# Fused pooled attention and branch mixture: other queues and order for the first keys and queries, and tile 1 done like tile 0

## The chip, the cores and the metric

The kernel runs on one NeuronCore of a Trainium2 chip. The metric is the device time of one execution in microseconds (us), lower is better. The profile gives a span, from the first to the last instruction of the core; the time of an execution is some 2 us longer.

## The reference

```python
# attention: q, k, v of shape (8, 8, 576, 64); keys and values are averaged over 8 neighbours
k_p = k.reshape(B, H, 72, 8, D).mean(axis=3)
v_p = v.reshape(B, H, 72, 8, D).mean(axis=3)
scores = (1 / sqrt(D)) * q @ k_p.transpose(0, 1, 3, 2)
attn = exp(scores - max(scores));  attn = attn / (sum(attn) + 1e-9)
x = (attn @ v_p)                       # -> (4608, 512): tokens by heads * head_dim
# mixture: 4 experts, w1 (4, 512, 1024), w2 (4, 1024, 512), p of shape (4608, 4)
p = domain_probs / (domain_probs.sum(-1) + 1e-9)
out = sum over e of p[:, e] * (relu(x @ w1[e]) @ w2[e])
```

## The kernel before

The 4,608 tokens are cut into 36 tiles of 128, four tiles to a group of 512. For each group and expert there is a step: `up` multiplies the group's turned tokens `xT` with one expert's `w1` (eight blocks of 128 columns, ReLU on ScalarE), and `down` multiplies the result, tile by tile, with `w2`; `collect` scales it on VectorE and adds it up. The main loop over 36 steps puts `up` of the next step between the `down` of this one, in an order written out by hand (`SLOTS`, `plan`), with the attention of later groups placed in its slots. Each engine runs its instructions in the order of the program.

Ahead of that loop stands a head, also in an order written out by hand, which makes the attention of group 0 (tiles 0 to 3) and the first expert's products for it. Its parts:

- `qg` (L129): the queries of all four tiles, 1 MB in F32, loaded by SP. `split_q(c)` (L565) casts one tile to BF16 on ScalarE, `turn_q` (L301) transposes it on TensorE and ScalarE copies it to `qT`. Tile `c` of group 0 holds every fourth token.
- `load_rows` (L77) loads the first keys into `kraw[0]` on GpSimd's queue, which casts to BF16, in three parts; `fold_keys0` (L581) adds eight neighbours on VectorE in three steps, `turn_keys0` transposes on TensorE, `take_keys0` (L601) copies into `kT[0]`. `load_v(0)` and then the weights follow on the same queue.
- `scores` (L316), `less_max` (L343: maxima and difference on VectorE), `expo` (L349, ScalarE).
- Tile 0 goes "in rows": `expo` writes `attn` unnormalised, `attn_T` (L387) transposes it and a copy makes `attnT`; `sums0` (L631) forms the sums over each head by products with the constant `own`; `context_rows` (L404) makes the context with tokens in partitions, and its division by the sums writes `x_sb`; `turn_x0` (L645) transposes it, and ScalarE copies it to `xT`.
- Tiles 1 to 3: `normalise` (L377) sums and divides on VectorE ahead of `attn_T`, and `context` (L424) gives `xT` turned.
- `up_tile(s, i)` (L460) is the up-projection for one tile alone, in two halves of 16 products.
- `idle_products(n)` (L569) runs `n` products on a tile of zeros whose result is not used.
- `own` and `ident` are made on GpSimd; `mask_v` (L184) is spread from `own` on VectorE.

PSUM pools hold two buffers each (`ps_h`, `ps_o`, `ps_t`) or one (`ps_s`, the scores), so a writer waits until the reader of an older tile is done.

The order of the head after the keys is:

```python
    take_keys0()
    make_mask_v()
    scores(0)
    split_q(2)
    turn_q(2)
    less_max(0)
    split_q(3)
    expo(0)
```

Of the kernel before, what the change touches and what calls it, by code (L numbers as in the profile page):

```python
# [10 lines left out]
ALU = mybir.AluOpType  # L11
AX = mybir.AxisListType
BF16 = mybir.dt.bfloat16
# [4 lines left out]
def kernel(  # L18
# [58 lines left out]
    def load_rows(dst, src, parts=((0, NB - 1),)):  # L77
        rows = src.rearrange("h (j r) d -> (h j) (r d)", r=POOL)
        for i0, i1 in parts:
            nc.gpsimd.dma_start(  # L80
                out=dst[:, i0:i1, :],
                in_=rows[i0 * P:i1 * P].rearrange("(i p) x -> p i x", p=P),
            )
        nc.gpsimd.dma_start(out=dst[0:TAIL, NB - 1, :], in_=rows[(NB - 1) * P:ROWS])
# [4 lines left out]
    def load_v(b):  # L89
        load_rows(vraw[b % 2], v[b])  # L90
# [22 lines left out]
    def load_w1(e):  # L113
        for half in range(2):
            cols = slice(half * (F // 2), (half + 1) * (F // 2))
            nc.gpsimd.dma_start(
                out=w1_sb[e][:, :, cols],
                in_=moe_w1[e].rearrange("(kc p) f -> p kc f", p=P)[:, :, cols],
            )

    def load_w2(e):
# [4 lines left out]

    qg = raw.tile([P, H, TPG, D], F32, name="qg")  # L129
    nc.sync.dma_start(  # L130
        out=qg[:], in_=q[0][:, 0:G, :].rearrange("h (p c) d -> p h c d", c=TPG)
    )
    dp0 = const.tile([P, TPG, E], F32, name="dp0")
    nc.sync.dma_start(
        out=dp0[:], in_=moe_domain_probs[0:G].rearrange("(p c) e -> p c e", c=TPG)
# [6 lines left out]

    still = const.tile([P, G], BF16, name="still")
    nc.vector.memset(still[:], 0.0)  # L144
    load_rows(kraw[0], k[0], ((0, 2), (2, 4)))
    load_v(0)
    ident = const.tile([P, P], BF16, name="ident")
    make_identity(nc, ident[:])

# [2 lines left out]
    for sign, base in ((1, 0), (-1, SP - 1)):  # L152
        nc.gpsimd.affine_select(
            out=own[:], in_=own[:], compare_op=ALU.is_ge, fill=0.0,
            base=base, channel_multiplier=sign,
            pattern=[[sign * (P - PW), NPAIR], [sign * P, 2], [-sign * SP, 2]],
        )
    load_w1(0)
    load_w2(0)
    load_w1(1)  # L160
# [133 lines left out]
    def by_dma(t):  # L294
        return t >= 2 * TPG


    def in_rows(t):
        return t == 0 or by_dma(t)

    def turn_q(t):  # L301
        qT[t] = qtp.tile([P, NPAIR, P], BF16, name="qT")
# [98 lines left out]

    def context_rows(t):  # L404
        ps = ps_t.tile([P, DM], F32, tag="t", name="x_ps")
        for b, _, n, at in segments(t * P, P):
            flat = vbd[b][:].rearrange("p a z y d -> p (a z y d)")
            for i in range(NB):
                c0, c1, h0 = chunk(i)
                nc.tensor.matmul(  # L410
                    ps[at:at + n, h0 * D:(h0 + c1 - c0) * D],
                    lhsT=attnT[t][:, i, at:at + n], rhs=flat[:, c0 * D:c1 * D],
                    start=(i == 0), stop=(i == NB - 1), skip_group_check=True,
                )
        x_sb = soft.tile([P, DM], BF16, name="x_sb")
        nc.vector.scalar_tensor_tensor(  # L416
            out=x_sb[:].rearrange("p (h d) -> p h d", d=D),
            in0=ps[:].rearrange("p (h d) -> p h d", d=D), scalar=V_MEAN,
            in1=rss[t][:].unsqueeze(2).to_broadcast([P, H, D]),
            op0=ALU.mult, op1=ALU.mult,  # L420
        )
        return x_sb

    def context(t):  # L424
        g, col = t // TPG, (t % TPG) * P
        if t % TPG == 0:
            xT[g] = grp.tile([P, KC, G], BF16, name="xT")
        if by_dma(t):
            x_sb = x_sbs[t] = context_rows(t)
            nc.sync.dma_start_transpose(out=xT[g][:, :, col:col + P], in_=x_sb[:])  # L430
            return
        ps = ps_t.tile([P, KC, P], F32, tag="t", name="x_ps")
        for pair in range(NPAIR):
            for b, _, n, at in segments(t * P, P):
                for z in range(2):
                    nc.tensor.matmul(  # L436
                        ps[:, pair, at:at + n],
                        lhsT=vbd[b][:, pair, z].rearrange("p y d -> p (y d)"),
                        rhs=attnT[t][:, pair + z, at:at + n],
                        start=(z == 0), stop=(z == 1),  # L440
                    )
        nc.scalar.copy(out=xT[g][:, :, col:col + P], in_=ps[:])  # L442
# [14 lines left out]
        nc.scalar.activation(out=hs[s][:, fb, :], in_=ps[:], func=ACT.Relu)  # L457


    def up_tile(s, i):  # L460
        g, e = divmod(s, E)
        if i == 0:
            hs[s] = hpool.tile([P, FB, G], BF16, name="h_sb")
        cols = slice(i * P, (i + 1) * P)
        for f0 in range(0, FB, TPG):
            ps = ps_h.tile([P, TPG, P], F32, tag="h", name="h_ps")
            for f in range(TPG):
                for kc in range(KC):
                    nc.tensor.matmul(  # L469
                        ps[:, f], lhsT=w1_sb[e][:, kc, (f0 + f) * P:(f0 + f + 1) * P],  # L470
                        rhs=xT[g][:, kc, cols], start=(kc == 0), stop=(kc == KC - 1),
                    )
            nc.scalar.activation(
                out=hs[s][:, f0:f0 + TPG, cols], in_=ps[:], func=ACT.Relu
            )
# [87 lines left out]


    def split_q(c):  # L565
        nc.scalar.copy(out=qrow[c][:], in_=qg[:, :, c, :])


    def idle_products(n):  # L569
        ps = ps_o.tile([P, DM], F32, name="o_ps")  # L570
        for _ in range(n):
            nc.tensor.matmul(ps[:], lhsT=still[:, 0:P], rhs=still[:], start=True, stop=True)  # L572
# [7 lines left out]

    def fold_keys0(p1, i0, i1):  # L581
        rows = kraw[0][0:p1, i0:i1]
        for n in (4, 2):
            w = n * D
            nc.vector.tensor_add(
                out=rows[:, :, 0:w], in0=rows[:, :, 0:w], in1=rows[:, :, w:2 * w]
            )
        twice = [p1, i1 - i0, 2, D]
        nc.vector.tensor_tensor(
            out=kpad0[0:p1, i0:i1], in0=rows[:, :, 0:D].unsqueeze(2).to_broadcast(twice),  # L590
            in1=rows[:, :, D:2 * D].unsqueeze(2).to_broadcast(twice), op=ALU.add,
        )
# [35 lines left out]
            )  # L628


    def sums0():  # L631
        ps = ps_o.tile([P, H], F32, tag="o_ps", name="es_ps")
        flat = own[:].rearrange("p a z y -> p (a z y)")
        for i in range(NB):
            c0, c1, h0 = chunk(i)
            nc.tensor.matmul(
                ps[:, h0:h0 + c1 - c0], lhsT=attnT[0][:, i], rhs=flat[:, c0:c1],
                start=(i == 0), stop=(i == NB - 1), skip_group_check=True,
            )
        es = soft.tile([P, H], F32, name="es")  # L640
        nc.vector.tensor_scalar_add(out=es[:], in0=ps[:], scalar1=1e-9)
        rss[0] = soft.tile([P, H], F32, name="rs")
        nc.vector.reciprocal(out=rss[0][:], in_=es[:])

    def turn_x0(x_sb):  # L645
        ps = ps_t.tile([P, KC, P], BF16, tag="t", name="xT_ps")
        for kc in range(KC):
            nc.tensor.transpose(ps[:, kc], x_sb[:, kc * P:(kc + 1) * P], ident[:])
        nc.scalar.copy(out=xT[0][:, :, 0:P], in_=ps[:])

    idle_products(14)
    split_q(0)
    split_q(1)
    turn_q(0)
    turn_q(1)
    for part in ((P, 0, 2), (P, 2, 4), (TAIL, 4, 5)):
        fold_keys0(*part)
        turn_keys0(*part)
        idle_products(2)
    take_keys0()  # L660
    make_mask_v()
    scores(0)
    split_q(2)
    turn_q(2)
    less_max(0)
    split_q(3)
    expo(0)
    idle_products(2)
    spread_values0(sum_values0())
    attn_T(0)  # L670
    scores(1)
    maxima(1)
    idle_products(2)
    sums0()
    turn_q(3)
    idle_products(1)
    xT[0] = grp.tile([P, KC, G], BF16, name="xT")
    x0 = context_rows(0)
    idle_products(4)
    turn_x0(x0)  # L680
    less(1)
    expo(1)
    idle_products(2)
    up_tile(0, 0)
    scores(2)
    normalise(1)
    idle_products(4)
    less_max(2)
    domain_probs0()
    for t in range(1, TPG):  # L690
        attn_T(t)
        if t + 1 < TPG:
            expo(t + 1)
        if t == 1:
            idle_products(3)
        else:
            down(0, t - 1, 0, FB // 2)
        context(t)
        if t == 1:
            scores(3)  # L700
            up_tile(0, t)
            down(0, t - 1)
        else:
            down(0, t - 1, FB // 2, FB)
            up_tile(0, t)
        if t + 1 < TPG:
            normalise(t + 1)
        if t == 1:
            less_max(3)
        if t == TPG - 1:  # L710
            make_mask_k()
        collect(0, t - 1)
    load_q(2 * TPG)
# [48 lines left out]
```

## Time and profile before

| what | value |
|---|---|
| median of 3 runs | 552.44 us (552.02 to 552.67) |
| profiled execution, its own time | 551.91 us |
| its span | 549.9 us |
| TensorE busy | 537.4 us, 98% |
| tile 0's `attnT` copy starts | 15.38 us |
| up-projection of tile 0, of tile 1, main loop's first product | 19.05, 24.45, 36.87 us |

All times are counted from the span's start. In the profile PE is TensorE's products, PEld its weight loads, DVE VectorE, ACT ScalarE, POOL GpSimd, SP the SyncE queue that starts transfers. Numbers such as L453 are lines of the kernel; those in the prediction are lines of the kernel before. A row of the timeline reads: start, duration, engine, line, operation, output and input, count.

### The profile page before, as it was taken

To read this page: it belongs to the slowest core of one execution; us is meant where nothing else is said; L and a number is where in the kernel's file an instruction comes from. 1 tells how busy PE (TensorE), PEld (TensorE's weight loads), DVE (VectorE), ACT (ScalarE), POOL (GpSimd) and SP (SyncE) were. 2 spreads that over 40 slices of the span, in tenths; PEclk is the share of its full clock that TensorE was granted. 3 is DMA by queue.
4 is the path that set the end of the run, shared out by engine and by line. 5 is a ranking of instruction groups with operands and counts; after the bars stand their busy time and mean duration, and the time that the engine had idled before them with its cause. 6 is when DMAs were issued, how large, how long until landed. Compare 5 with 4: busy or idle time off the path is not lost.

```text
span 549.9 us, 7267 instructions
## 1 busy us (share of the span) xinstructions
PE 537.4 (98%) x2873; PEld 260.8 (47%) x2929; DVE 264.7 (48%) x456; ACT 213.5 (39%) x355; POOL 70.7 (13%) x120
## 2 busy tenths in 40 slices
PE   7899999999999999999999999999999999999997
PEld 2664554444444444444444444444444444444443
DVE  4874847444744446544554444744473444422223
ACT  3554653333333333333333333333333333333330
POOL 7234001121111100012011100101010000000000
PEclk9999999999999999999999999999999999999999
DMA  9999926556645563367435543335333521111002
GB/s 196 206 202 198 201 19 130 83 67 88 119 72 76 79 121 73 52 83 91 110 54 76 83 108 39 52 42 114 45 54 41 92 57 32 21 39 38 1 1 76
DMA packets 110689, 45.84 MB, mean 83 GB/s; under 512 B 87584, under 2 KB 106016, under 8 KB 110656
## 3 DMA queue, kind: packets, MB, share of 16 engines
q0 software_dynamic: 51472, 22.03, 32.6%
q1 hardware_dynamic: 59184, 23.35, 17.9%
q8 instruction: 23, 0.38, 0.3%
q14 instruction: 10, 0.08, 0.0%
HBM read 45.16 MB, written 9.44 MB: 99 GB/s over the span
## 4 chain that ended last, share of the span: by engine, by line
PE 96%; DMA 1%; DVE 1%; issue 1%; ACT 1%; POOL 0%; POOLq 0%
PE o_ps L486 45%; PE h_ps L453 44%; PE x_ps L410 2%; PE sc L320 2%; PE h_ps L469 1%; DMA kraw<-in_k_dram 1%; PE x_ps L436 1%; PE o_ps L572 0%; PE at_ps L394 0%; ACT attnT L395 0%; PE qT_ps L310 0%; POOL kraw L80 0%; DVE mx L334 0%; DVE d_sb L338 0%; DVE acc L501 0%
## 5 line engine op out<-in xcount | busy, mean ns | idle before, releaser
L457 ACT ACTIVATE h_sb<-h_ps 128x512 bf16<-128x512 f32 x280 | 167.1, 597 | 296.5 <-PE h_ps L453 292.3
L453 PE MATMUL h_ps<-xT,w 128*128 128x512 bf16 x1088 | 271.8, 379 | 1.5
L486 PE MATMUL o_ps<-w,h_sb 128*128 128x512 bf16 x1130 | 270.0, 379 | 1.3
L486 PEld LDWEIGHTS <-h_sb 128*128 128x128 bf16 x1152 | 112.4, 98 | 133.8
L501 DVE SCALAR_TENSOR_TENSOR acc<-o_ps,p_sb,acc 128x512 f32<-128x512 f32 x108 | 81.0, 750 | 180.4 <-PE o_ps L486 177.7
L453 PEld LDWEIGHTS <-w 128*128 128x128 bf16 x1120 | 105.9, 98 | 116.9
L497 DVE TENSOR_SCALAR acc<-o_ps,p_sb 128x512 f32<-128x512 f32 x36 | 27.0, 750 | 60.8 <-PE o_ps L486 60.8
L525 POOL COPY gated<-x_sb 1x1 bf16<-1x1 bf16 x28 | 7.8, 278 | 367.7 <-DVE x_sb L416 367.7
L108 POOL DMA_DIRECT2D qrow<-in_q_dram x36 | 30.5, 850 | 26.3 <-DMA w<-in_moe_w_dram 14.8
L334 DVE TENSOR_REDUCE mx<-sc 128x8 f32<-128x576 f32 x36 | 27.2, 756 | 10.8 <-PE sc L320 10.6
L338 DVE TENSOR_TENSOR d_sb<-sc,mx 128x576 f32<-128x576 f32 x36 | 27.3, 757 | 1.2
L416 DVE SCALAR_TENSOR_TENSOR x_sb<-x_ps,rs 128x512 bf16<-128x512 f32 x29 | 20.1, 692 | 12.5 <-PE x_ps L410 12.1
L351 ACT ACTIVATE attn<-d_sb 128x576 bf16<-128x576 f32 x29 | 19.8, 682 | 3.7 <-DVE d_sb L338 0.5
L372 DVE TENSOR_REDUCE es<-attn 128x8 f32<-128x576 bf16 x28 | 20.8, 744 | 0.0
L410 PEld LDWEIGHTS <-attnT 128*128 128x128 bf16 (+1 forms) x160 | 12.2, 100 | 7.3 <-issue 1.3
L320 PE MATMUL sc<-kT,qT 128*128 128x144 bf16 (+1 forms) x160 | 15.0, 227 | 0.2 <-DVE kT L609 0.2
L320 PEld LDWEIGHTS <-qT 128*128 128x128 bf16 (+1 forms) x160 | 11.1, 100 | 8.4 <-issue 2.2
L410 PE MATMUL x_ps<-vbd,attnT 128*128 128x192 bf16 (+5 forms) x160 | 14.7, 231 | 0.0
L572 PE MATMUL o_ps<-still 128*128 128x512 bf16 x36 | 11.4, 435 | 1.4 <-DVE still L144 1.3
L235 DVE TENSOR_TENSOR vraw<-vraw 128x1280 bf16<-128x1280 bf16 (+1 forms) x14 | 9.2, 654 | 0.2
L235 DVE TENSOR_TENSOR kraw<-kraw 128x1280 bf16<-128x1280 bf16 (+1 forms) x14 | 9.0, 640 | 0.2
L469 PE MATMUL h_ps<-xT,w 128*128 128x128 bf16 x128 | 7.8, 219 | 0.7 <-ACT xT L442 0.4
(76 smaller groups left out, 148.8 us busy)
## 6 DMA issues: line engine op xcount, KB each, us to landing
out_dram<-acc SPq DMA_DIRECT2D x36, 256.0 KB, 2.2
vraw<-in_v_dram POOLq DMA_DIRECT2D x8, 512.0 KB, 6.7
w<-in_moe_w_dram POOLq DMA_DIRECT2D x8, 512.0 KB, 16.1
w<-in_moe_w_dram POOLq DMA_DIRECT2D x4, 1024.0 KB, 16.2
kraw<-in_k_dram POOLq DMA_DIRECT2D x7, 512.0 KB, 6.2
qrow<-in_q_dram POOLq DMA_DIRECT2D x28, 128.0 KB, 4.0
qg<-in_q_dram SPq DMA_DIRECT2D x1, 1024.0 KB, 5.8
kraw<-in_k_dram POOLq DMA_DIRECT2D x2, 256.0 KB, 6.7
```

What stands on the lines that cost most here:

```text
L108: nc.gpsimd.dma_start(out=qrow[t][at:at + n], in_=q[b][:, tok:tok + n, :].rearrange("h p d -> p h d"),)
L320: nc.tensor.matmul(sc[at:at + n, pair // 2, (pair % 2) * PW:(pair % 2 + 1) * PW], lhsT=qT[t][:, pair, at:at + n], rhs=kT[b][:].rearrange(" ...
L334: nc.vector.reduce_max(out=mxs[t][:], in_=by_head(t), axis=AX.X)
L338: nc.vector.tensor_tensor(out=st[t][:], in0=by_head(t), in1=mxs[t][:].unsqueeze(3).to_broadcast([P, 2, 4, SP]), op=ALU.subtract,)
L372: nc.vector.reduce_sum(out=es[:], in_=e, axis=AX.X)
L410: nc.tensor.matmul(ps[at:at + n, h0 * D:(h0 + c1 - c0) * D], lhsT=attnT[t][:, i, at:at + n], rhs=flat[:, c0 * D:c1 * D], start=(i == 0), s ...
L416: nc.vector.scalar_tensor_tensor(out=x_sb[:].rearrange("p (h d) -> p h d", d=D), in0=ps[:].rearrange("p (h d) -> p h d", d=D), scalar=V_ME ...
L453: nc.tensor.matmul(ps[:], lhsT=w1_sb[e][:, kc, fb * P:(fb + 1) * P], rhs=xT[g][:, kc, :], start=(kc == 0), stop=(kc == KC - 1),)
L457: nc.scalar.activation(out=hs[s][:, fb, :], in_=ps[:], func=ACT.Relu)
L486: nc.tensor.matmul(ps[:], lhsT=hs[s][:, fb, i * P:(i + 1) * P], rhs=w2_sb[e][:, fb, :], start=(fb == 0), stop=(fb == FB - 1),)
L497: nc.vector.tensor_scalar_mul(out=accs[t][:], in0=ps[:], scalar1=p_sb[:, e, t:t + 1])
L501: nc.vector.scalar_tensor_tensor(out=accs[t][:], in0=ps[:], scalar=p_sb[:, e, t:t + 1], in1=accs[t][:], op0=ALU.mult, op1=ALU.add,)
```

## The change

The first keys no longer go through GpSimd's queue: SP loads them in F32 into a new tile `kf`, the short last part first, and then the queries of tile 0 alone (`qf`). The queries of tiles 1 to 3 (`qg`) are loaded by GpSimd's queue in BF16, behind the values and ahead of the weights; the constants `ident` and `own` are made ahead of these loads. The first step of the fold reads `kf` and writes `kraw[0]`. `mask_v` is made first.

Tile 1 is done in rows too: `sums0` becomes `sums_by_products(t)`, `context_rows` can write x in two halves (two divisions on VectorE), and `turn_x0` becomes `turn_x(t, halves)`, with two transposes and a copy for each half, in two PSUM pools. `up_tile` can run one of its halves; the turn of tile 1's exponents, copied on VectorE, stands between the halves for tile 0. `scores(3)` comes after `up_tile(0, 1)`. There are 30 idle products instead of 38.

```diff
-    qg = raw.tile([P, H, TPG, D], F32, name="qg")
-    nc.sync.dma_start(
-        out=qg[:], in_=q[0][:, 0:G, :].rearrange("h (p c) d -> p h c d", c=TPG)
-    )
+    kf = raw.tile([P, NB, POOL * D], F32, name="kf")
+    rows0 = k[0].rearrange("h (j r) d -> (h j) (r d)", r=POOL)
+    nc.sync.dma_start(out=kf[0:TAIL, NB - 1, :], in_=rows0[(NB - 1) * P:ROWS])
+    for i in (0, 2):
+        nc.sync.dma_start(
+            out=kf[:, i:i + 2, :],
+            in_=rows0[i * P:(i + 2) * P].rearrange("(i p) x -> p i x", p=P),
+        )
+    q0 = q[0][:, 0:G, :].rearrange("h (p c) d -> p h c d", c=TPG)
+    qf = raw.tile([P, H, D], F32, name="qf")
+    nc.sync.dma_start(out=qf[:], in_=q0[:, :, 0, :])
...
-    load_rows(kraw[0], k[0], ((0, 2), (2, 4)))
-    load_v(0)
     ident = const.tile([P, P], BF16, name="ident")
     make_identity(nc, ident[:])
...
+    load_v(0)
+    qg = raw.tile([P, H, TPG - 1, D], BF16, name="qg")
+    nc.gpsimd.dma_start(out=qg[:], in_=q0[:, :, 1:TPG, :])
     load_w1(0)
...
     def in_rows(t):
-        return t == 0 or by_dma(t)
+        return t < 2 or by_dma(t)
...
+        x = [soft.tile([P, n * D], BF16, name=f"x_sb{i}of{parts}") for i in range(parts)]
+        for i in range(parts):
+            heads = slice(i * n, (i + 1) * n)
+            nc.vector.scalar_tensor_tensor(
...
     def split_q(c):
-        nc.scalar.copy(out=qrow[c][:], in_=qg[:, :, c, :])
+        nc.scalar.copy(out=qrow[c][:], in_=qg[:, :, c - 1, :] if c else qf[:])
...
+    def turn_x(t, halves):
+        n = KC // 2
+        for i, pool, tag in ((0, ps_t, "t"), (1, ps_h, "h")):
+            ps = pool.tile([P, n, P], BF16, tag=tag, name="xT_ps")
+            for kc in range(n):
+                nc.tensor.transpose(
+                    ps[:, kc], halves[i][:, kc * P:(kc + 1) * P], ident[:]
+                )
+            nc.scalar.copy(
+                out=xT[0][:, i * n:(i + 1) * n, t * P:(t + 1) * P], in_=ps[:]
+            )
+        idle_products(1)
```

The head's order, after the change:

```python
    idle_products(14)
    make_mask_v()
    split_q(0)
    for part in ((TAIL, 4, 5), (P, 0, 2)):
        fold_keys0(*part)
        turn_keys0(*part)
    idle_products(3)
    turn_q(0)
    fold_keys0(P, 2, 4)
    turn_keys0(P, 2, 4)
    take_keys0()
    idle_products(3)
    scores(0)
    less_max(0)
    split_q(1)
    expo(0)
    idle_products(2)
    v_ps = sum_values0()
    idle_products(1)
    turn_q(1)
    spread_values0(v_ps)
    attn_T(0)
    scores(1)
    split_q(2)
    maxima(1)
    idle_products(2)
    xT[0] = grp.tile([P, KC, G], BF16, name="xT")
    sums_by_products(0)
    x_sb = context_rows(0, 2)
    turn_q(2)
    split_q(3)
    idle_products(1)
    turn_x(0, x_sb)
    less(1)
    expo(1)
    up_tile(0, 0, (0,))
    attn_T(1, copy=nc.vector.tensor_copy)
    up_tile(0, 0, (TPG,))
    sums_by_products(1)
    x_sb = context_rows(1, 2)
    scores(2)
    turn_q(3)
    idle_products(2)
    turn_x(1, x_sb)
    less_max(2)
    expo(2)
    domain_probs0()
    up_tile(0, 1)
    scores(3)
    down(0, 0)
    normalise(2)
    less_max(3)
    collect(0, 0)
    for t in range(2, TPG):     # as before
```

More of the change, by code (lines that the diff above doesn't have):

```diff
@@ L398, in chunk, with context_rows @@
         return max(0, 4 * i - 1), min(4 * NPAIR, 4 * i + 2), max(0, 2 * i - 1)
-    def context_rows(t):
+    def context_rows(t, parts=1):
         ps = ps_t.tile([P, DM], F32, tag="t", name="x_ps")
@@ L414, in context_rows @@
                 )
[L415 to L422, printed above, removed]
+        n = H // parts
+        x = [soft.tile([P, n * D], BF16, name=f"x_sb{i}of{parts}") for i in range(parts)]
+        for i in range(parts):
+            heads = slice(i * n, (i + 1) * n)
+            nc.vector.scalar_tensor_tensor(
+                out=x[i][:].rearrange("p (h d) -> p h d", d=D),
+                in0=ps[:].rearrange("p (h d) -> p h d", d=D)[:, heads], scalar=V_MEAN,
+                in1=rss[t][:, heads].unsqueeze(2).to_broadcast([P, n, D]),
+                op0=ALU.mult, op1=ALU.mult,
+            )
+        return x
     def context(t):
@@ L428, in context @@
         if by_dma(t):
-            x_sb = x_sbs[t] = context_rows(t)
+            (x_sb,) = context_rows(t)
+            x_sbs[t] = x_sb
             nc.sync.dma_start_transpose(out=xT[g][:, :, col:col + P], in_=x_sb[:])
@@ L457, in up, with up_tile @@
         nc.scalar.activation(out=hs[s][:, fb, :], in_=ps[:], func=ACT.Relu)
-    def up_tile(s, i):
+    def up_tile(s, i, starts=tuple(range(0, FB, TPG))):
         g, e = divmod(s, E)
-        if i == 0:
+        if s not in hs:
             hs[s] = hpool.tile([P, FB, G], BF16, name="h_sb")
         cols = slice(i * P, (i + 1) * P)
-        for f0 in range(0, FB, TPG):
+        for f0 in starts:
             ps = ps_h.tile([P, TPG, P], F32, tag="h", name="h_ps")
@@ L582, in fold_keys0 @@
         rows = kraw[0][0:p1, i0:i1]
+        src = kf[0:p1, i0:i1]
         for n in (4, 2):
@@ L585, in fold_keys0 @@
             nc.vector.tensor_add(
-                out=rows[:, :, 0:w], in0=rows[:, :, 0:w], in1=rows[:, :, w:2 * w]
+                out=rows[:, :, 0:w], in0=src[:, :, 0:w], in1=src[:, :, w:2 * w]
             )
+            src = rows
         twice = [p1, i1 - i0, 2, D]
@@ L628, in spread_values0, with sums_by_products @@
             )
-    def sums0():
+    def sums_by_products(t):
         ps = ps_o.tile([P, H], F32, tag="o_ps", name="es_ps")
@@ L636, in sums0 @@
             nc.tensor.matmul(
-                ps[:, h0:h0 + c1 - c0], lhsT=attnT[0][:, i], rhs=flat[:, c0:c1],
+                ps[:, h0:h0 + c1 - c0], lhsT=attnT[t][:, i], rhs=flat[:, c0:c1],
                 start=(i == 0), stop=(i == NB - 1), skip_group_check=True,
@@ L641, in sums0 @@
         nc.vector.tensor_scalar_add(out=es[:], in0=ps[:], scalar1=1e-9)
[L642 to L649, printed above, removed]
+        rss[t] = soft.tile([P, H], F32, name="rs")
+        nc.vector.reciprocal(out=rss[t][:], in_=es[:])
@@ L651 @@
+    def turn_x(t, halves):
[8 more added lines that the diff above has]
+                out=xT[0][:, i * n:(i + 1) * n, t * P:(t + 1) * P], in_=ps[:]
+            )
+        idle_products(1)
     idle_products(14)
+    make_mask_v()
@@ L652 @@
     split_q(0)
[L653 to L656, printed above, removed]
+    for part in ((TAIL, 4, 5), (P, 0, 2)):
         fold_keys0(*part)
         turn_keys0(*part)
-        idle_products(2)
+    idle_products(3)
+    turn_q(0)
+    fold_keys0(P, 2, 4)
+    turn_keys0(P, 2, 4)
     take_keys0()
-    make_mask_v()
+    idle_products(3)
     scores(0)
-    split_q(2)
-    turn_q(2)
     less_max(0)
-    split_q(3)
+    split_q(1)
     expo(0)
     idle_products(2)
-    spread_values0(sum_values0())
+    v_ps = sum_values0()
@@ L670 @@
+    idle_products(1)
+    turn_q(1)
+    spread_values0(v_ps)
     attn_T(0)
     scores(1)
+    split_q(2)
     maxima(1)
     idle_products(2)
-    sums0()
-    turn_q(3)
+    xT[0] = grp.tile([P, KC, G], BF16, name="xT")
+    sums_by_products(0)
+    x_sb = context_rows(0, 2)
+    turn_q(2)
+    split_q(3)
     idle_products(1)
[L677 to L680, printed above, removed]
+    turn_x(0, x_sb)
     less(1)
     expo(1)
+    up_tile(0, 0, (0,))
@@ L683 @@
+    attn_T(1, copy=nc.vector.tensor_copy)
+    up_tile(0, 0, (TPG,))
+    sums_by_products(1)
+    x_sb = context_rows(1, 2)
+    scores(2)
+    turn_q(3)
     idle_products(2)
[L684 to L687, printed above, removed]
+    turn_x(1, x_sb)
     less_max(2)
+    expo(2)
     domain_probs0()
-    for t in range(1, TPG):
+    up_tile(0, 1)
+    scores(3)
+    down(0, 0)
+    normalise(2)
+    less_max(3)
+    collect(0, 0)
+    for t in range(2, TPG):
         attn_T(t)
@@ L693 @@
             expo(t + 1)
[L694 to L697, printed above, removed]
+        down(0, t - 1, 0, FB // 2)
         context(t)
[L699 to L705, printed above, removed]
+        down(0, t - 1, FB // 2, FB)
+        up_tile(0, t)
         if t + 1 < TPG:
             normalise(t + 1)
-        if t == 1:
-            less_max(3)
-        if t == TPG - 1:
+        else:
             make_mask_k()
```

## The prediction

> **What bounds the kernel now.** I read the engines' busy shares first, then the chain that ended last, then the head's instructions in order of time, and last the same stretch in half-microsecond windows for the transfers.
>
> ```profile
> PE 537.4 (98%) x2873; PEld 260.8 (47%) x2929; DVE 264.7 (48%) x456; ACT 213.5 (39%) x355; POOL 70.7 (13%) x120
> ...
> PE 96%; DMA 1%; DVE 1%; issue 1%; ACT 1%; POOL 0%; POOLq 0%
> ```
>
> TensorE is busy 98% of the span. What the change can move is the head, where the chain leaves TensorE; after it the products stand back to back, so the kernel ends sooner by as much as the main loop (`up`, L453) starts sooner. The chain by time:
>
> ```profile
> 2.16 6.94 DMA kraw<-in_k_dram
> ...
> 11.84 0.69 DVE mask_v L185
> ...
> 12.56 0.77 DVE mx L334
> ...
> 15.38 0.70 ACT attnT L395
> ...
> 19.05 1.95 PE h_ps L469 x32
> ...
> 24.45 1.95 PE h_ps L469 x32
> ```
>
> The first 9 us are a wait for the keys; then come tile 0's softmax, its first up-projection at 19.05 and tile 1's at 24.45. In the timeline the main loop's first product is at 36.87. So I measure three distances: the copy `attnT` of tile 0 at 15.38; from there 3.67 to 19.05; 5.40 to 24.45; 12.42 to 36.87.
>
> Why the keys come late stands in the transfers (columns: window, PE, PEld, DVE, ACT and POOL busy, clock, DMA share, GB/s):
>
> ```profile
> 2.00:2.50 0.50, 0.50 (x2) 0.15 (x1) 0.11 (x1) 0.09 (x1) 0.50 (x2) 1.00 0.56 80
> 3.00:3.50 0.50, 0.50 (x3) 0.22 (x2) 0.00 (x0) 0.00 (x0) 0.50 (x2) 1.00 0.98 307
> 5.00:5.50 0.50, 0.50 (x4) 0.20 (x2) 0.00 (x0) 0.00 (x0) 0.41 (x3) 1.00 1.14 346
> 8.00:8.50 0.50, 0.25 (x4) 0.07 (x2) 0.47 (x2) 0.50 (x2) 0.50 (x2) 1.00 1.23 199
> ```
>
> GB/s counts bytes written (the page gives the casting queue 22.03 MB, with 45.16 MB read). All windows up to 5.5 sum to 1,008 KB, about the 1,049 KB of `qg` alone, which landed at 6.6. So the keys on GpSimd's queue, issued at 1.33, moved almost nothing until SP's queue was drained; from 6.0 on that queue, which casts to BF16, writes 199 to 215 GB/s. With 590 KB of keys and 590 KB of values from 6.0 at 205 KB/us I get 11.75; the values' products start at 12.89 after a wait, a landing lag of 1.1 us.
>
> **SP's queue after the change.** Keys in F32 (131, 524 and 524 KB), then tile 0's queries (262 KB). By the same cumulative windows (130 KB at 3.0, 639 at 4.5, then 390 KB/us) they end at about 3.0, 4.55 and 5.9. The queries go in 1,024 pieces of 256 bytes, which no SP load of before has. Lower bound: by bytes, 0.67. Upper bound: each piece as dear as one of `qg`'s 1,024 bytes, 1,049/390 = 2.7. The row with the same pieces at the source is GpSimd's `qrow` load of 128 KB: 4.0 us to landing against 2.2 for SP's 256 KB stores, so at most about 1.8 for 1,024 pieces. I take 1.1: queue drained at 7.0, queries landed at 7.7 (`qg` lagged 0.7).
>
> The Trainium skill, "DMA: Bandwidth & Descriptors", Specifications, speaks against these pieces: below 512 bytes a transfer does not reach line rate. No SP load of before shows that; as an estimate, at half of the pace above, the queries would take 1.34 us. The same page, "Queues, rings and completion order", says that each DMA engine goes round between its queues; the 1,008 KB above speak against an even share here. By that rule the values would move earlier and the queries later, with the same sum of bytes at the end.
>
> **Tile 0 up to the exponent.** ScalarE casts the queries (0.62, L566), TensorE turns them and the last keys (about 0.35), VectorE takes the keys out (0.6, L609): `scores(0)` at about 9.6, against 11.86. The F32 fold costs 0.69 for 128x512 (row L416, same shape) instead of 0.43, but that part is folded by 8.0 while TensorE, in order, waits for the queries until 8.4; cover 0.4, and beyond it 1:1. `mask_v` (0.69) goes to the start of VectorE's list, where it waits for `own` on GpSimd (1.33 plus 1.3 of `ident` and `own` = 2.7) and ends at 3.4, ahead of the first keys; it also no longer stands before the maxima. Maxima and difference, 0.76 each, end at about 11.6.
>
> But ScalarE must first run `split_q(1)`, which stands ahead of `expo(0)` and waits for the other queries. These are third on GpSimd's queue: values 590 KB from 7.0, 2.9 us; then 393 KB in 1,024 pieces, by bytes 1.9. Between 1.8 us for 1,024 pieces of 256 source bytes and 5.1 for 1,024 of 2,048 (the values' pace), 768 bytes give 2.7. I take 2.1, near the bytes, because the loads of large pieces run by bytes. With the lag of 1.1 they land at L = 7.0 + 2.9 + 2.1 + 1.1 = 13.1. So the scores' 2 us are mostly lost: the new wait on ScalarE has `expo(0)`, the copy of `qT(1)` and `attnT` queued behind it, and TensorE's `turn_q(1)`, `attn_T(0)` and `scores(1)` behind those. Casts overlap by 0.1 (two took 1.14): exponent from L + 0.56 to L + 1.25, tile 0 turned by TensorE (0.45 and gaps), `attnT` at L + 1.78 = 14.9, 0.5 earlier than 15.38.
>
> **From `attnT` to the main loop.** Sums on TensorE, reciprocal on VectorE ready 1.57 after A (the start of `attnT`); the two halves of x cost 0.43 each (0.16 + 256 of 0.53/512) against 0.69 for one, the second ending 0.38 after the first. The changed program lets the first half's transposes wait for ScalarE's copy of `qT(2)` (A + 2.26), so that half gains little there. ScalarE then does `split_q(3)` (0.62) and two xT copies of 0.37 instead of one 0.58; but the up-projection starts on the first. It starts at U = A + 3.1 instead of 3.67: 0.55 saved.
>
> Tile 1 done like tile 0 drops `normalise` (0.75 + 0.17 + 0.20 + 0.76 on VectorE, between exponent and turn) for five products and a division on x. Half an up-projection (0.94), turn (0.28), VectorE's copy 0.49 (row L269) under the other half (0.9), sums at U + 2.2, reciprocal at U + 2.95, halves until U + 3.75, transposes and copies: `up_tile(0, 1)` at U + 4.56 instead of 5.40: 0.84 saved. Here `scores(3)` moves behind it: 0.25 back, with small gaps 0.3. Idle products removed (38 to 30) stood beside VectorE's work. I add 0.2 for gaps between steps, since adding up before in this way comes out 0.2 short. Sum: 0.55 + 0.84 - 0.3 - 0.2 = 0.9, and 0.5 from L: 1.4 us. Break-even is L = 14.5.
>
> Edits at nothing: `dp0` and `dpr` go behind keys and queries on SP, but are read at 22.98 and 35.95. The first weights stand behind 983 KB instead of 1,180, from 7.0 instead of 6.0: level. The second half of w1 lands at about 18.3 and is needed at 19.0; slipping with L, its need slips too.
>
> **Level.** The profiled execution took 551.91 with a span of 549.9, 2.0 around it; the median shown, 552.44, is 0.53 above. Minus 1.4: 550.5 for such an execution, 551.0 for the median. A comparison can tell 0.2%, 1.1 us.
>
> **Rivals.** (1) Slower: GpSimd's query pieces cost by count, not by bytes, 5.1 instead of 2.1 us. L = 16.1, 1.6 later than break-even: 554.0. It decides from 3.5 us on. For it: the 128 KB loads take 4.0 us to land. Against: a 1,024-byte written piece is 2.7 times as large.
> (2) Tile 1's gain hidden: ScalarE, with two casts, the turned queries' copy and four xT copies, ends last instead of VectorE, and the 0.9 goes. Only L counts: 552.44 - 0.5 = 551.9. For it: ScalarE's order is the longest from A to U.
> (3) Faster: pieces by bytes and the keys' lag of 0.56 (7.84 against 6.0 + 1.28): L = 6.55 + 2.9 + 1.9 + 0.6 = 11.95, gain 2.5, 549.9. If the queries come before 11.0, the softmax ends last instead.
>
> **How the numbers follow.** Forecast 0.60 (0.52 of it over 1.1 us faster, 0.08 less), rival 3 0.08, rival 2 0.19, rival 1 0.13. Faster 0.60, same 0.08 + 0.19 = 0.27, slower 0.13. The range goes from just below rival 3, 549.6, past rival 2 to 553.0, the half-way point of rival 1 (L = 15.1, +0.6); rival 1's full price is left out.
>
> **What would show it.** Right: ScalarE's longest head wait is before the second cast, for the queries, ending near 13; `scores(0)` near 9.6; `attnT` near 14.9; up-projections near 18.0 and 22.6; first main-loop product near 35.5. Wrong: the cast released before 11, values' products later than 12.9, tile 0's queries after 9.5, or TensorE's products 0.43 apart again, as before 4.7, after one of the new gaps.

## The result and the profile after

The changed kernel is slower: 555.06 us in the median of 9 runs (553.24 to 555.94) against 551.99 (551.71 to 552.67) for the kernel before in the same comparison. The ratio of the mean times is 1.0045 with a 95% interval of 1.0033 to 1.0058. The forecast was 551.0, and the range ended at 553.0. The profiled execution took 554.46, with a span of 552.2. One execution of experiment 5 below ran at a granted clock (the share of its full speed that TensorE is given) of 0.752 throughout and is left out of all figures.

TensorE's busy time, from the page, is within 0.4 us of before, and the chain that ended last gains a percent of DMA:

```profile
PE 537.8 (97%) x2871; PEld 261.6 (47%) x2927; DVE 265.2 (48%) x458; ACT 213.0 (39%) x356; POOL 70.0 (13%) x118
...
PE 96%; DMA 2%; issue 1%; ACT 1%; DVE 0%; SPq 0%; DVEq 0%
```

So most of the time was lost in front of TensorE's work. The chain in order of time (start, duration, what) names the transfer:

```profile
2.56 9.38 DMA qf<-in_q_dram
...
11.96 0.63 ACT qrow L578
...
12.64 0.56 PE qT_ps L318 x4
...
14.69 0.48 PE sc L328 x4
...
21.35 0.27 PE h_ps L481 x2
...
25.95 0.27 PE h_ps L481 x2
```

Tile 0's queries, the 262 KB that stand behind the keys on SP's queue, landed at 11.94 instead of the forecast 7.7. Three rows of the timeline show what followed:

```profile
14.48 0.69 PE L328 MATMUL sc<-kT,qT 128*128 128x144 bf16 x4
...
18.19 0.70 ACT L403 COPY attnT<-at_ps 128x640 bf16<-128x640 bf16 x1
...
38.77 5.34 PE L465 MATMUL h_ps<-xT,w 128*128 128x512 bf16 x23
```

`scores(0)` starts at 14.48 (forecast 9.6; the chain's row shows only the part from 14.69), `attnT` of tile 0 at 18.19 (forecast 14.9, before 15.38), the main loop at 38.77 (forecast 35.5, before 36.87). The waits of the first 45 us (who waited for what: total, times, longest) say who stood behind it:

```profile
ACT qrow L578 <- DMA qf<-in_q_dram: 9.9, 1, 9.9
...
PE qT_ps L318 <- ACT qrow L578: 4.9, 1, 4.9
...
ACT qrow L578 <- DMA qg<-in_q_dram: 0.9, 1, 0.9
```

ScalarE waited 9.9 us for tile 0's queries and only 0.9 for the other queries, which I had expected to be its longest head wait. TensorE stood still for 4.9 us. The half-microsecond windows (PE, PEld, DVE, ACT and POOL busy, granted clock of TensorE with 1.00 for full speed, DMA share, GB/s) show what that cost besides, and where the queries were meanwhile:

```profile
6.00:6.50 0.50, 0.50 (x4) 0.12 (x2) 0.32 (x2) 0.00 (x0) 0.50 (x2) 1.00 0.86 199
...
7.00:7.50 0.50, 0.50 (x5) 0.12 (x2) 0.47 (x2) 0.00 (x0) 0.50 (x1) 1.00 0.88 103
...
12.50:13.00 0.50, 0.36 (x5) 0.37 (x6) 0.00 (x0) 0.08 (x1) 0.18 (x1) 0.73 1.58 192
13.50:14.00 0.50, 0.50 (x2) 0.15 (x1) 0.49 (x2) 0.32 (x1) 0.50 (x2) 0.50 1.32 204
...
16.50:17.00 0.50, 0.50 (x6) 0.36 (x4) 0.26 (x1) 0.21 (x1) 0.00 (x0) 1.00 1.26 209
```

At 6.0 SP's queue moves 199 GB/s; at 7.0 both queues together move only 103, and after that the rate is almost all GpSimd's. And after the standstill the granted clock is 0.50 from about 12.7 to 16.1, so tile 0's scores ran at half pace.

The transfers' records show the same piece by piece. Pieces of 256 bytes (SP, tile 0's queries) and of 1,024 written bytes (GpSimd) that started in each half microsecond:

| from, us | 256 B | 1,024 B |
|---|---|---|
| 5.5 | 102 | 0 |
| 6.0 | 380 | 0 |
| 6.5 | 211 | 12 |
| 7.0 | 110 | 23 |
| 8.0 | 47 | 60 |
| 9.0 | 19 | 65 |
| 10.0 | 19 | 87 |

Alone on the DMA engines 380 small pieces started in half a microsecond, at 18 ns each. When GpSimd's pieces (about 97 ns each at full pace) arrived at 6.7, 430 of the 1,024 had not started, and the last of them ended at 11.5.

The start times say how the two queues share. From 9 to 10 us the small pieces start in four evenly spaced series (9.03, 9.13, 9.24, 9.34 and so on is one): in each, one piece every 105 ns, a little more than one of GpSimd's pieces takes. This fits turns of one piece each, one small piece for each large one. That each series is one DMA engine is an inference, since the records do not name the engine.

### The profile page after: what moved, and what is told of

It reads as the page before. It is cut to its first block, busy times and chain, and to the rows that moved or that the text cites. A ratio compares the mean times of both kernels' runs of the same rounds, so it can differ in the third digit from the quotient of the medians.

```text
span 552.2 us, 7269 instructions
## 1 busy us (share of the span) xinstructions
PE 537.8 (97%) x2871; PEld 261.6 (47%) x2927; DVE 265.2 (48%) x458; ACT 213.0 (39%) x356; POOL 70.0 (13%) x118
## 4 chain that ended last, share of the span: by engine, by line
PE 96%; DMA 2%; issue 1%; ACT 1%; DVE 0%; SPq 0%; DVEq 0%
PE o_ps L498 45%; PE h_ps L465 44%; PE x_ps L418 2%; PE sc L328 2%; DMA qf<-in_q_dram 2%; PE h_ps L481 1%; PE x_ps L448 1%; PE o_ps L584 1%; PE qT_ps L318 0%; PE at_ps L402 0%; PE v_ps L629 0%; ACT qT L322 0%; SPq L133 0%; PE xT_ps L664 0%; DVE acc L513 0%
## 5 line engine op out<-in xcount | busy, mean ns | idle before, releaser
L537 POOL COPY gated<-x_sb0of 1x1 bf16<-1x1 bf16 x28 | 7.8, 279 | 367.9 <-DVE x_sb0of L427 367.9
L427 DVE SCALAR_TENSOR_TENSOR x_sb0of<-x_ps,rs 128x512 bf16<-128x512 f32 (+1 forms) x30 | 20.2, 674 | 12.4 <-PE x_ps L418 11.7
L359 ACT ACTIVATE attn<-d_sb 128x576 bf16<-128x576 f32 x30 | 20.5, 683 | 4.7 <-DVE d_sb L346 1.4
L318 PE MATMUL qT_ps<-ident,qrow 128*128 128x128 bf16 x36 | 3.6, 226 | 5.0 <-ACT qrow L578 4.9
```

What stands on the lines that cost most here:

```text
L359: nc.scalar.activation(out=attn[t % 2][:, 0:ROWS].rearrange("p (h j) -> p h j", j=SP), in_=st[t][:].rearrange("p g h j -> p (g h) j"), fun ...
```

## The experiments

Two theories stood for the late landing. **Sharing:** the two queues take turns on each DMA engine, so every small piece that is left waits behind a large one. **Slow pieces:** 1,024 pieces of 256 bytes take that long by themselves. Beside these the half clock and tile 1's part had to be priced. Unless a diff says otherwise, a kernel is the changed one with the edit shown. The median of before was 551.92 in the comparison of the first four, 551.91 and 551.85 in the later two.

**1. GpSimd's queue held until the queries are in.**

```diff
+    gate0 = const.tile([1, 1], F32, name="gate0")
+    nc.gpsimd.tensor_copy(out=gate0[:], in_=qf[0:1, 0, 0:1])
     load_v(0)
```

> The changed kernel, but GpSimd copies one element of tile 0's queries before it issues the values, so that its queue moves nothing until those queries have landed. Theory (the two queues share the DMA engines piece by piece, and tile 0's 256-byte pieces lose against the 2 KB reads of GpSimd's queue): the queries land near 7.7 us instead of 11.94, scores(0) start near 10; the values come later (near 12.5) and the other queries near 15.5. Rival (256-byte pieces are slow by themselves): the queries land near 11.9 all the same.

The chain:

```profile
2.57 4.83 DMA qf<-in_q_dram
...
8.99 7.43 DMA qg<-in_q_dram
...
16.45 0.63 ACT qrow L580
...
18.46 0.69 ACT attnT L405
```

Two rows of the timeline, the scores and the values' products:

```profile
9.31 0.41 PE L330 MATMUL sc<-kT,qT 128*128 128x144 bf16 x4
...
14.07 1.81 PE L631 MATMUL v_ps<-vraw,ident 128*128 128x320 bf16 x8 [3.92 <-DMA vraw<-in_v_dram]
```

With nothing beside them the same pieces in the same place landed at 7.42, 4.5 us earlier, and `scores(0)` started at 9.31. The small pieces are not slow by themselves, and the forecast's own figure (7.7) was right for this case. One run took 555.51, since values (14.07) and other queries (16.42) now come later than in the changed kernel (12.8 and 14.7), and later than the 12.5 and 15.5 expected; the clock was down as well, from 14.6 to 21.5. The other queries landed 2.4 us after TensorE had stopped waiting for the values, so their price of 2.1 was about right and rival 1's 5.1 was not.

**2. Tile 0's queries ahead of the keys on SP.**

```diff
+    qf = raw.tile([P, H, D], F32, name="qf")
+    nc.sync.dma_start(out=qf[:], in_=q0[:, :, 0, :])
     nc.sync.dma_start(out=kf[0:TAIL, NB - 1, :], in_=rows0[(NB - 1) * P:ROWS])
...
-    nc.sync.dma_start(out=qf[:], in_=q0[:, :, 0, :])
```

> The changed kernel with one move: SP loads tile 0's queries ahead of the keys, so that the small pieces run before GpSimd's data begins at 6.5 us. Sharing theory: queries land by 5, the last keys between 7 and 8.3, scores(0) near 10, TensorE stays at full clock; the other queries then hold the exponent, attnT of tile 0 starts near 15.3 and the time is about 1 us below the kernel before, 3.5 to 4 below the changed one. Rival (small pieces slow by themselves, 6 us): queries land near 8, the last keys near 11.5, scores(0) not before 13.5, the time stays at the changed kernel's, 2 to 3 us above before.

Two rows of the timeline, the cast of the queries and the fold of the last keys to arrive, and below them that fold in the changed kernel:

```profile
4.09 0.62 ACT L578 CAST qrow<-qf 128x512 bf16<-128x512 f32 x1 [2.00 <-DMA qf<-in_q_dram]
...
9.97 0.69 DVE L598 TENSOR_TENSOR kraw<-kf 128x512 bf16<-128x512 f32 x1 [1.74 <-DMA kf<-in_k_dram]
```

```profile
6.62 0.69 DVE L598 TENSOR_TENSOR kraw<-kf 128x512 bf16<-128x512 f32 x1 [0.27 <-DMA kf<-in_k_dram]
```

The queries landed at 4.09. Now the last part of the keys shares with GpSimd's queue and was late instead: 9.97, against 6.62 in the changed kernel and later than the 7 to 8.3 expected. These keys are 3.35 us later; the queries are 7.9 earlier. About half of the 3.35 is the place behind the queries: the two parts ahead, which were in when GpSimd's data had hardly begun, are already 1.6 and 1.9 later (folded at 5.17 and 6.89 against 3.56 and 5.01). In the profiled execution the clock stayed at 1.00 and `attnT` came at 15.63. The median of 553.02 is 2.0 below the changed kernel, but 1.1 above before (1.0019, 1.001 to 1.0028), where about 1 below was expected.

**3. TensorE kept busy through the wait.**

```diff
-    idle_products(3)
+    idle_products(23)
     turn_q(0)
```

> The changed kernel with 23 instead of 3 idle products ahead of the turn of tile 0's queries, so that TensorE is not idle for the 4.9 us in which it waits for them. Theory (the idle time lowers the clock, granted 0.5 from 12.6 to 16.2 us): the granted clock stays at 1.0, scores(0) start 1.95 to 2.05 after the queries land instead of 2.52, attnT of tile 0 about 0.9 earlier than 18.19, and the time is 0.7 to 1.2 us below the changed kernel's. Rival (the clock costs nothing, since VectorE and ScalarE carry the chain): the time is the changed kernel's.

The chain, for the same three steps:

```profile
11.98 0.63 ACT qrow L578
...
13.87 0.42 PE sc L328 x4
...
20.26 0.27 PE h_ps L481 x2
```

The copy, from the timeline:

```profile
17.13 0.69 ACT L403 COPY attnT<-at_ps 128x640 bf16<-128x640 bf16 x1
```

The queries were as late as before (11.98), the clock stayed at 1.00, the four products of the scores took 0.41 in the timeline instead of 0.69, `attnT` came at 17.13, 1.06 earlier, and the up-projection 1.09 earlier. So the half clock cost 1.1 us of the head in the changed kernel's profiled execution. The median was 554.08, but its ratio of 1.0043 (1.003 to 1.0057) overlaps the changed kernel's 1.0045: the time alone does not resolve it. In the trace the lead of 1.09 lasts to 208 us, and 0.65 of it is gone at 309, a stretch in which TensorE waited 0.2 for keys turned by DMA; that was in this one execution and is not explained.

**4. Tile 1's part alone,** with the loads and the order up to the exponent of before (against the kernel before: `in_rows(t)` for `t < 2`, `sums_by_products`, `turn_x` and what follows it as in the change).

> The kernel before with the second part of the change alone: tile 1 in rows like tile 0, x in halves, the order behind the sums of tile 0 as in the changed kernel; loads, queues and the order up to there as before. Theory (my step from attnT to the main loop was right): attnT of tile 0 at 15.4, up-projection of tile 0 some 3.1 later, of tile 1 4.6 after that, the main loop 0.9 us earlier than 36.87 and the time 0.9 us below the kernel before. Rival (ScalarE's longer list takes it back): the main loop starts at 36.9 or later, time within 0.3 us of before.

The chain up to the first up-projection, and from the timeline that of tile 1 and the start of the main loop:

```profile
15.32 0.70 ACT attnT L395
...
18.33 0.27 PE h_ps L473 x2
```

```profile
22.60 2.17 PE L473 MATMUL h_ps<-xT,w 128*128 128x128 bf16 x32
...
35.48 5.34 PE L457 MATMUL h_ps<-xT,w 128*128 128x512 bf16 x23
```

3.01 from `attnT` instead of 3.67, then 4.27 instead of 5.40. The median is 550.95, ratio 0.9982 (0.9973 to 0.9991): 0.97 faster than before, with 0.9 forecast for this part. It beats both kernels. But the main loop starts 1.39 earlier, not 0.9, and the span is 1.37 shorter (548.6). The time gains less because an execution of this kernel takes 2.4 us longer than its span and one of the kernel before 2.0; all kernels with tile 1 in rows show 2.1 to 2.5, those with tile 1 as before 1.8 to 2.0. Nothing here shows why.

**5. The loads alone,** with tile 1 done as before.

> The changed loads, the early mask and the head's order up to tile 0's exponent, with tile 1 done as before. If the two parts of the change add up, the median is the changed kernel's 555.06 plus the 0.97 that tile 1's part brought alone: 556.0 us. The load part then costs 4.1 us against before. The rival is that tile 1's part is worth more behind a late attnT than behind an early one, or less (its steps wait for the same late queries): then the time is more than 0.6 us away from 556.0. Tile 0's queries land at 11.9 and attnT starts at 18.2 in both theories.

Its three executions took 556.35 to 557.17, in the median 556.42: 0.4 more than the sum of the parts, less than the 0.6 that the rival asks for. (The 556.8 of the next expectation is the median of all four.) The ratio of 1.0084 (1.0069 to 1.01) has the sum of the parts, 1.0074, inside its interval, so the times do not decide. The load part costs 4.5 us against before. A second run gave a trace.

> The loads alone once more, for its trace at the full clock: its median of 556.8 was 0.8 above the sum of the parts, and its times were all at a mean clock of 0.993. If the extra is the clock, TensorE's products before the main loop run at half pace longer than the 3.5 us (12.5 to 16.0) of the changed kernel; if it is tile 1's part being worth more behind a late attnT, the clock is as in the changed kernel and the up-projection of tile 1 starts more than 5.4 us after that of tile 0.

```profile
18.77 0.70 ACT L403 COPY attnT<-at_ps 128x640 bf16<-128x640 bf16 x1
...
22.84 1.95 PE L481 MATMUL h_ps<-xT,w 128*128 128x128 bf16 x32
...
28.58 1.95 PE L481 MATMUL h_ps<-xT,w 128*128 128x128 bf16 x32 [0.56 <-ACT xT L454]
```

This run took 556.22. The clock was back by 16.6, after 3.2 us of products at half pace, about as in the changed kernel, so it is not the extra. The distances are 4.07 and 5.74, each longer than before's 3.67 and 5.40. Taken to the same place, tile 1's up-projection, tile 1's part is worth 2.05 behind late queries (4.07 + 5.74 against 3.16 + 4.60) and 1.79 behind early ones (3.67 + 5.40 against 3.01 + 4.27); from `attnT` to the main loop it is 1.64 and 1.33. So it is worth some 0.3 more behind a late `attnT`: the direction of the second theory, at half of its 0.6. The queries landed at 12.6 in this run, 0.7 later yet.

**6. Tile 0's queries alone on SP,** and the keys back on GpSimd's queue, folded and turned in the order of before.

```diff
-    nc.sync.dma_start(out=kf[0:TAIL, NB - 1, :], in_=rows0[(NB - 1) * P:ROWS])
...
+    load_rows(kraw[0], k[0], ((0, 2), (2, 4)))
     ident = const.tile([P, P], BF16, name="ident")
...
-        src = kf[0:p1, i0:i1]
+        src = rows
```

> The changed kernel with the keys back on GpSimd's queue in BF16, ahead of the constants and values; SP loads only tile 0's queries, as its first load, and the other queries stay behind the values. If SP's queue and GpSimd's take turns by pieces, 262 KB on SP are done by about 4 us and keep the keys back only until then: queries landed at 4.1, keys at 5.1, 6.4 and 6.7, scores(0) about 8.6, values about 10, other queries about 12.0 and then the last ones before the first exponent of tile 0; attnT of tile 0 about 13.8, and about 549.6 us. The rival is that GpSimd's first data come no earlier than 5.1 whatever SP has queued (its own start-up): keys at 7.8 as before, other queries at 13, attnT about 14.8, 550.7 us. By the prediction's rule that GpSimd's queue waits until SP's is drained, it is the first of the two.

The chain:

```profile
6.26 7.63 DMA qg<-in_q_dram
13.89 0.02 issue
13.91 0.62 ACT qrow L571
...
15.66 0.70 ACT attnT L396
...
18.79 0.27 PE h_ps L474 x2
```

Neither theory had it: 551.96 in the median, ratio 1.0004 (0.9994 to 1.0013). In the transfers' records GpSimd's first pieces start at 3.2, while SP's are still starting (until 3.5), and 80 of them start in the half microsecond from 4.5, so they do come earlier than 5.1 and without waiting for SP's queue to be empty; but the first keys are folded at 7.34, only 0.5 earlier than the 7.84 of before, and the other queries landed at 13.89, not 12.0. They held the exponent, and `attnT` came 1.77 after them: the forecast's L + 1.78 is seen here as it was meant.

**7. The same, with the cast and turn of tile 1's queries behind `attn_T(0)`.**

```diff
-    split_q(1)
     expo(0)
...
-    turn_q(1)
     spread_values0(v_ps)
     attn_T(0)
+    split_q(1)
+    turn_q(1)
     scores(1)
```

> The kernel with tile 0's queries alone on SP (551.96, attnT of tile 0 at 15.66, other queries landed at 13.89), with the cast and the turn of tile 1's queries moved from ahead of tile 0's exponent to behind attn_T(0). Nothing then holds the exponent but the softmax, whose difference ended at 13.36: exponent from 13.4, attnT at about 14.65, 1.0 earlier. If attnT alone sets what follows, as the prediction's step 'from attnT to the main loop' has it, the up-projections follow at 3.1 and 7.7 from it (17.75, 22.35) and the median is 551.0. The rival is that scores(1), now behind a later cast, becomes last in tile 1's chain and takes it back: up-projection of tile 0 about 18.3, of tile 1 24.0, and 552.8.

Three rows of the timeline:

```profile
14.20 0.69 ACT L396 COPY attnT<-at_ps 128x640 bf16<-128x640 bf16 x1 [0.55 <-PE at_ps L395]
...
17.00 0.76 DVE L335 TENSOR_REDUCE mx<-sc 128x8 f32<-128x576 f32 x1 [2.80 <-PE sc L321]
...
20.30 1.22 PE L474 MATMUL h_ps<-xT,w 128*128 128x128 bf16 x16
```

`attnT` was 1.46 earlier, and the up-projection 1.51 later than in experiment 6: 553.08. In TensorE's order the sums of tile 0 stand behind `scores(1)`, which waited for the later cast, and TensorE's gaps around 14 to 16 us then cost the clock as well (0.50 from about 17.1 to 20.5), though none of its waits there is longer than 1.3 us. The rival holds in direction and size, though not in its place: the loss is already there at tile 0's up-projection, 20.30 where 18.3 was expected.

**8. Experiment 4 with the mask made first.**

```diff
+    make_mask_v()
     split_q(0)
...
     take_keys0()
-    make_mask_v()
     scores(0)
```

> Before's loads with tile 1's part, and the mask made at the head of VectorE's list instead of between the keys' copy and the maxima. The mask took 0.69 us of VectorE and stood at 11.84, beside scores(0) (0.5 us on TensorE), so what it can give back is what it outlasts the scores by: maxima 0.2 to 0.3 us earlier, attnT 15.0 to 15.1 instead of 15.32, and the median 0.3 below the 550.95 of tile 1's part alone: 550.7. The rival is that the maxima wait for scores(0) on TensorE anyway: 550.95.

The scores and the maxima here, from the chain, and in experiment 4, from the timeline:

```profile
12.01 0.42 PE sc L320 x4
...
12.46 0.77 DVE mx L334
```

```profile
11.81 0.41 PE L320 MATMUL sc<-kT,qT 128*128 128x144 bf16 x4 [0.18 <-DVE kT L615]
...
12.51 0.76 DVE L334 TENSOR_REDUCE mx<-sc 128x8 f32<-128x576 f32 x1
```

The maxima follow the scores' start by 0.45 here, by 0.70 in experiment 4: 0.25 saved. The keys landed 0.2 later in this profiled execution, which hides it in the absolute times. The median of 550.54, ratio 0.9975 (0.9964 to 0.9985), is 0.41 below experiment 4 and the best of all, but the two intervals overlap, so only the gain over before is settled by the times.

## Why the prediction was wrong, point by point

**The step that failed** is the price of tile 0's queries on SP's queue: 1.1 us, drained at 7.0, landed at 7.7. It was right for the pieces alone (7.42 in experiment 1) and 4.2 short beside GpSimd's queue (11.94), where the same pieces ran from 5.7 to 11.5, 5.8 us. I had read the 1,008 KB by 5.5 us of before as an order, "GpSimd's queue moves nothing until SP's is drained", and on that ground set aside the rule that speaks for sharing. What the row showed was a late start: with a megabyte or more queued on SP, GpSimd's first pieces came 3.9 us (before) and 4.6 us (after) after their issue, against 1.8 us in experiment 6 and 1.6 us in experiment 1. Once started, they share, by the four series above one piece in turn. In before the start fell at the end of SP's transfer and was not told apart from an order; the change put the queries' small pieces just there. The Trainium skill, "DMA: Bandwidth & Descriptors", "Queues, rings and completion order", says that each engine goes round between its queues; experiments 1 and 2 agree. I had noted that by this rule the values would move earlier and the queries later "with the same sum of bytes at the end", and left it there; but what stands first in the chain is the queries' landing, not the sum.

**The second term, not in the sum at all,** is the clock: 1.1 us (experiment 3). The prediction named products 0.43 apart as a sign of being wrong, but put no price on it, since its TensorE was to wait only until 8.4. The times of experiment 2 bear the size out: its two executions at a mean clock of 0.999 took 551.88 and 552.04, the six at 0.997 took 552.55 to 553.28, the two at 0.992 and 0.994 took 554.15 and 554.22. One stretch of 3.41 us at half speed takes 0.003 off the mean, so each such stretch goes with about 1 us.

**The bill.** Forecast for `attnT` 14.9, measured 18.19: 3.3 more. Of this 2.2 is the landing (experiment 3's `attnT` at 17.13 less 14.9) and 1.1 the clock. The landing itself was 4.2 late; 2.0 of that was covered, since the forecast's exponent was to be held by the other queries until 13.1 anyway. From `attnT` to the main loop the change won 0.91 (21.49 before, 20.58 after), so the main loop came 1.90 late, and the profiled execution 2.55. The 3.07 between the medians has more of the clock in it: four of the nine executions, the profiled one among them, had a mean clock of 0.996 to 0.997 and took 553.24 to 554.46; five had 0.994, which is two stretches at half speed, and took 555.06 to 555.94. No trace shows where the second one lay.

**L.** The other queries landed at 14.7 (forecast 13.1), because the values were in at about 12.8 (forecast 11.0). It made no difference: their cast was done at 15.34, while the softmax's difference ended only at 16.76. The wait that I had called the new one on ScalarE exists (experiments 1 and 6), but in the changed kernel another ended last.

**Right:** the small pieces' own time (1,024 of 18 ns on 16 engines are 1.15 us, and in experiment 1 they ran from 5.7 to 7.0; forecast 1.1, and 1.34 as the estimate at half pace), the distance from `attnT` to the first up-projection (forecast 3.1, measured 3.16), from there to tile 1's (4.56, 4.60), L + 1.78 (1.77), the 2.1 for the other queries' pieces (2.1 in experiment 6, from the values' landing at 11.82), the F32 folds at 0.69 behind a cover, the mask's place. That tile 1's part alone brought 0.97, with 0.9 forecast, is partly luck: the main loop gained 1.39, and 0.4 of it was lost outside the span, which the prediction put at 2.0 as before. One reading of before was also wrong: the transfers' records do show an SP load in short pieces, the 64-byte ones of `dp`, at 11 ns each against 46 for `qg`'s 1,024 bytes.

**The rivals.** Rival 1 had the sign and nearly the number (554.0), but by pieces that cost by count; those cost 2.1. Rival 2 is refuted by experiment 4, rival 3 by every landing (the other queries were in at 13.5 at the earliest, not at 11.95). The mechanism that decided was in none of them.

**Open:** why SP's backlog delays GpSimd's first pieces, and why an execution of the kernels with tile 1 in rows takes some 0.4 us more outside its span. The page of the Trainium skill named above, in the same section, gives a packet of some 9 to 17 descriptors for each turn; the series in the changed kernel step by one piece, and for this case that measurement decides.

## What to carry to other kernels

A transfer that is needed first must not be the tail of one queue when another queue wakes up beside it: price it once alone and once in turn with the other's pieces, by the number of its pieces, and put small pieces first. Before a row of transfers is read as "queue B waits for queue A", look whether B had started at all. And where a head leaves TensorE mostly idle for some 3.4 us, put the half clock into the sum: ahead of the four falls seen here its products filled 0.09 to 1.62 us of the last 3.41.

## What the runs showed of the hardware

- Two queues share DMA engines one piece in turn: 1,024 pieces of 256 bytes landed at 7.42 alone and at 11.94 beside GpSimd's pieces of 1,024 written bytes, in the same place of SP's queue. Late in that load they start 105 ns apart in each of four series, beside pieces of 97 ns; in experiment 3 the last ones start 58 ns apart, beside pieces of 384 bytes and 51 ns.
- GpSimd's queue starts later when SP's is full: first pieces 1.6 us after the issue with SP's queue empty, 1.8 with 262 KB on it, 3.9 to 4.6 with a megabyte or more.
- The granted clock falls to 0.50 after TensorE has had little work for a while: it held through the 4.9 us of the changed kernel and fell as work began again (about 12.7 to 16.1), but was down already at 10.0 in experiment 5's second run, while TensorE still stood. In experiment 1 it was down for 6.8 us (14.6 to 21.5), in experiment 7 for 3.4, there after waits of at most 1.3 us. In the 3.41 us ahead of each fall TensorE was busy for 0.09 us (changed kernel), 0.56 (experiment 1), 1.37 (experiment 7) and 1.62 (experiment 5). In these four traces every stretch between two changes of the clock is a multiple of 3.41 us. The Trainium skill, "TensorE: Matmul & The Clock Gate", "Part 1: The HAM clock gate", gives a free-running window of about 3.4 us; the 3.4 of the changed kernel and of experiment 7 agree with one such window and the 6.8 with two. That the window runs free would fit the different delays; no run here tests it.
